# Two channel quarters of one block go by one-pass products of halves, with the rest of a handwritten order rearranged

## The chip, the cores and the metric

One core of a Trainium2 chip runs the whole program in one launch. The metric is the device time of an execution in microseconds; the kernel before took 228.07 us in the median of three runs (226.97 to 228.76). The core's engines are TensorE (PE, with its weight loads as PEld), VectorE (DVE), ScalarE (ACT), GpSimd (POOL) and SyncE (SP), which issues the DMAs here.

## The reference, cut to what matters

A state-space scan over 4 batches of 8 heads, 768 tokens, is followed by a token mixer of rank 32 and a channel mixer. In the second part, per batch,

```
h  = x.T @ U @ V                    # 768 -> 32 -> 768 over tokens
u  = x + h.T                        # (768, 256)
ch = relu(u @ w_ch1) @ w_ch2        # 256 -> 1024 -> 256
out = u + ch                        # float32
```

and x is the scan's output with heads and head channels put side by side. The weights arrive as float64 and are turned into float32 on the chip.

## The kernel before, in words

Everything is issued in the order of one string, PLAN. Each word is a letter with indices, and calls one small function; the engines take their instructions in that order, each in a queue of its own, with semaphores between them where data or buffers require it. No time stands in the plan.

The scan goes by 12 pairs of 128-token blocks, three pairs a batch. For pair k: `L` loads its B, C and x (SP; a load is held until the last VectorE instruction ahead of it in the plan is done), `P` scales B and C (VectorE), `T` transposes them (TensorE, then three ScalarE copies; two words), `g` forms the products C·B in four PSUM banks, `m` and `M` mask two of these banks each (VectorE), `s` and `u` update the state (TensorE; VectorE, then a GpSimd multiplication, L567), `n` is the part inside a chunk (L633), `i` and `j` the two parts from the state (L611). Before `j` a one-column GpSimd copy (L574, tile `settled`) waits for the products of `n` and `i`, and the products of `j` wait for that copy. `y` takes the result from PSUM (two ScalarE copies), `t` transposes it to tokens.

The mixer of batch b has `p`, `q` and `a` (rank-32 token mixing; `a` ends in two VectorE additions into u), and then a channel mixer by blocks j of 384 tokens, channels m of 128 (8 of them, in four quarters of two), and output blocks k of 128 tokens:

- Batches 1 to 3 use halves. A number x is split into near = x·(1 - 2^-13) rounded to fp32r, far = x - near, and a third operand joined from both. `S` does so for u (a ScalarE copy at L722, two VectorE passes over 128x768). `f` (four products and a ScalarE scaling, L732) and `e` (two products and a ScalarE relu into near, L761) make one channel of the first layer; `h` takes far from PSUM and, after each second channel, joins (VectorE). `d b.j.k.n` is piece n of six of the second layer: near, far and joined halves against the three forms of the weights, four channels a piece, with a scaling of the bank after piece 3 and a product for the mixed tokens, an addition and the output's DMA after piece 5.
- Batch 0 uses plain float32: `U` makes a channel of the first layer into a tile gT (relu by ScalarE, L744), and `d` has four pieces, one quarter (two channels) each. All products of both kinds are issued at L727.

Weights: `c` (three steps) turns a tile of words into float32, `R` (two steps for w_ch1, three for w_ch2; R4 to R7 are the quarters of w_ch2) makes the three forms. The third form of a w_ch2 quarter takes the place of its float32 form, so R's third step must come after the last plain product with that quarter.

PSUM has two banks for each of the tags w, x, y and z. `f`, `U` and `a` use x or z, `g` two of each, a `d` block one (x, z, x for k = 0, 1, 2; y in the last three blocks). A bank is used again after `h` (for f and e), the mask (for g) or the addition (for d and a) has read it. All VectorE instructions carry line L158, that of a recording helper.

Of the kernel before, what the change touches and what calls it, by code (L numbers as in the profile page):

```python
# [22 lines left out]
AF = mybir.ActivationFunctionType
ALU = mybir.AluOpType
# [16 lines left out]
    'c0 i3 c2 b5.2 b5.0 q0 P4 j3 y3 W2 W3 b5.1 W4 a0.0 c2 a0.1 T4 T4 w5 c3 c3 c3 x4.0 U0.0.0 P5 '  # L41
    'U0.0.1 U0.1.1 R0 B6 t3 X5 g4 m4 T5 M4 T5 c5 c5 U0.1.0 c5 X6 U0.1.3 c4 c4 s4 u4 w6 w7 w8 U0.0.3 '
    'P6 U0.0.2 c6 U0.0.6 s5 c4 U0.1.7 c6 U0.1.2 u5 R0 R2 U0.1.6 n4 s6 L7 i4 g5 c6 R4 j4 y4 u6 T6 T6 '
    'm5 R2 R1 U0.0.4 M5 U0.1.4 n5 i5 L8 g6 c7 c7 c9 c9 j5 P7 T7 T7 M6 c7 t4 y5 U0.0.7 c8 U0.0.5 t5 '
    'm6 n6 R3 c9 P8 c8 p1 R7 g7 m7 L9 i6 M7 T8 T8 c8 q1 d0.0.2.0 d0.0.2.1 U0.1.5 a1.1 R1 d0.0.2.2 '
    'd0.0.2.3 a1.0 d0.0.1.0 R3 d0.0.1.1 d0.0.1.2 d0.0.0.0 d0.0.0.1 S1.0 f1.0.0 R7 d0.0.0.2 f1.0.1 '
    'd0.0.0.3 e1.0.0 h1.0.0 R5 d0.0.1.3 f1.0.6 R6 e1.0.1 d0.1.0.0 f1.0.7 P9 d0.1.0.1 h1.0.1 e1.0.6 '
    'd0.1.0.2 L10 R6 h1.0.6 e1.0.7 s7 u7 h1.0.7 f1.0.3 f1.0.2 d0.1.0.3 e1.0.2 d0.1.1.0 P10 h1.0.2 '
    'e1.0.3 h1.0.3 d0.1.2.0 f1.0.4 d0.1.1.1 R4 R4 f1.0.5 d0.1.1.2 d0.1.1.3 e1.0.4 e1.0.5 d0.1.2.1 '
    'd0.1.2.2 h1.0.4 h1.0.5 R6 d0.1.2.3 s8 j6 g8 y6 u8 s9 m8 n7 i7 S1.1 f1.1.0 f1.1.2 j7 y7 u9 M8 '  # L50
    't6 R5 e1.1.0 h1.1.0 n8 i8 T9 T9 t7 R5 d1.0.1.0 d1.0.1.1 d1.0.1.2 d1.0.0.0 d1.0.0.1 d1.0.0.2 '
    'd1.0.0.3 e1.1.2 R7 f1.1.3 d1.0.0.4 d1.0.0.5 d1.0.1.3 j8 y8 s10 d1.0.2.0 e1.1.3 h1.1.2 h1.1.3 '
# [12 lines left out]
    'f3.0.6 e3.0.0 h3.0.0 e3.0.1 d2.1.1.0 f3.0.3 d2.1.1.1 d2.1.1.2 d2.1.1.3 h3.0.1 f3.0.2 d2.1.1.4 '
    'e3.0.6 h3.0.6 e3.0.2 h3.0.2 d2.1.1.5 e3.0.3 h3.0.3 d2.1.0.5 f3.0.4 f3.0.5 f3.0.7 e3.0.4 h3.0.4 '
    'e3.0.5 d3.0.2.0 e3.0.7 d3.0.1.0 d3.0.2.1 d3.0.2.2 h3.0.5 d3.0.1.1 d3.0.1.2 S3.1 f3.1.4 f3.1.1 '
    'h3.0.7 d3.0.2.3 d3.0.1.3 f3.1.0 e3.1.4 h3.1.4 d3.0.2.4 e3.1.0 d3.0.2.5 e3.1.1 f3.1.5 d3.0.0.0 '
    'f3.1.2 d3.0.0.1 d3.0.0.2 d3.0.0.3 e3.1.2 h3.1.0 h3.1.1 f3.1.3 e3.1.5 h3.1.5 h3.1.2 d3.0.0.4 '
    'f3.1.6 e3.1.3 h3.1.3 d3.0.0.5 f3.1.7 d3.0.1.4 d3.0.1.5 e3.1.6 h3.1.6 e3.1.7 h3.1.7 d3.1.1.0 '  # L70
    'd3.1.1.1 d3.1.1.2 d3.1.1.3 d3.1.2.0 d3.1.2.1 d3.1.1.4 d3.1.1.5 d3.1.2.2 d3.1.2.3 d3.1.0.0 '
    'd3.1.0.1 d3.1.0.2 d3.1.0.3 d3.1.2.4 d3.1.2.5 d3.1.0.4 d3.1.0.5 ')


@with_exitstack
def kernel(
# [27 lines left out]
    nc = tc.nc  # L104
    P = 128
# [12 lines left out]
    NQ = NM // 2  # L118
# [28 lines left out]
    class Kept:  # L147
# [15 lines left out]
    vector = Kept(nc.vector)  # L163
# [7 lines left out]
        out=a_sb,  # L171
# [51 lines left out]
    w2f, w2b = {}, {}  # L223
# [102 lines left out]
    R = NB * NH * NC // 2  # L326
    la_ps = bank("w", 2, R)
    for g in range(2):
# [3 lines left out]
        out=la.rearrange("p b c h -> p b h c"),  # L332
        in0=la_ps.rearrange("p g (b h c) -> p (g b) h c", h=NH, c=NC),
# [337 lines left out]
    def mixer(b):  # L671
# [59 lines left out]
        def scaled(t):  # L731
            nc.scalar.activation(t, t, AF.Copy, scale=1.0 + EPS)  # L732
# [30 lines left out]
        def third(j, m):  # L763
# [5 lines left out]
            if m % 2:  # L769
                joined(near, far, both)  # L770

        def down(j, k, n):

            parts = b or j >= PLAIN
            pieces = 6 if parts else 4

            def weight(v, m):
                return w2[v][:, m] if v < 2 else w2b[m // 2][:, m % 2]

            if n == 0:  # L780
                gs["o", j, k] = bank(TAGS.get((b, j), "xzx")[k], DM)
            t = gs["o", j, k]
            c = HS // P * j + k
            if parts:
                v, half = divmod(n, 2)
                products(t, [(gs[j, m // 2][v][:, m % 2, ts(k, P)], weight(v, m))
                             for m in range(NQ * half, NQ * half + NQ)], n == 0)
                if n == 3:
                    scaled(t)
            else:  # L790
                products(t, [(gT[j, n][:, m, ts(k, P)], w2f[n][:, m]) for m in range(2)], n == 0)
            if n == pieces - 1:
# [57 lines left out]
    def ytokens_kept(k):  # L850
# [61 lines left out]
```

## Time and profile before

| | |
|---|---|
| median of three runs | 228.07 us |
| profiled execution: time, span | 227.86 us, 226.1 us |
| TensorE: matmuls, busy | 3012, 216.1 us (96%) |
| VectorE, ScalarE, GpSimd busy | 157.6, 114.3, 14.3 us |
| granted TensorE clock | 1.00 throughout |
| chain that ended last: TensorE's share | 89% |
| HBM read, written | 10.98 MB, 3.15 MB |

The span runs from the first instruction to the last; the time has a little around it. "Busy" unites overlapping instructions, and matmuls overlap in the profile, so the step from one matmul's start to the next is the better measure of what it costs. The plan's words can be told in the time line by their tiles: `x<-w2c,words` is a down piece of plain float32 (or of joined halves later), `x<-u,w` belongs to f or e, `y<-T,Sm` to i or j, `y<-M,x` to n. Waits are told as "idle before, and who ended it".

### The profile page before, as it was taken

The page shows a single profiled execution, that of the slowest core. Times are in us where ns is not written, and L with a number is a line of the kernel's source. Part 1 is how long each engine was busy: PE and PEld are TensorE (multiplying, and loading weights), DVE is VectorE, ACT ScalarE, POOL GpSimd, SP SyncE. Part 2 cuts the span into 40 slices and gives each one's busy share as a digit, 9 for nine tenths or more (in the row PEclk, how much of TensorE's full clock was granted, in tenths as well). Part 3 has the DMA queues.
Part 4 walks back from the last instruction along what each step waited for, and adds up shares of the span by engine and source line. Part 5 has one row for each costly group of instructions (what it writes and reads, how often), then busy time and mean ns, then how long its engine had stood idle before and what let it go on. Part 6 is the DMA issues. An engine that isn't in the chain of part 4 may idle for free.

```text
span 226.1 us, 7010 instructions
## 1 busy us (share of the span) xinstructions
PE 216.1 (96%) x3012; PEld 182.6 (81%) x3012; DVE 157.6 (70%) x331; ACT 114.3 (51%) x260; POOL 14.3 (6%) x37
## 2 busy tenths in 40 slices
PE   7889889999999999999999999999999999999993
PEld 4556645556678898997899898897998999999993
DVE  4675789899998866969816775667447974774921
ACT  3334856866995446333544532466237545655410
POOL 3020110012100000202101000100000000000000
PEclk9999999999999999999999999999999999999999
DMA  6997996887654402600001602000010000100011
GB/s 85 126 102 151 157 160 196 158 155 243 86 78 53 69 4 61 100 23 26 3 26 36 107 0 73 3 3 3 1 53 19 0 0 26 46 0 28 28 42 46
DMA packets 69518, 14.56 MB, mean 64 GB/s; under 512 B 63792, under 2 KB 67696, under 8 KB 69488
## 3 DMA queue, kind: packets, MB, share of 16 engines
q1 hardware_dynamic: 69488, 14.13, 34.0%
q8 instruction: 23, 0.38, 0.7%
q14 instruction: 7, 0.06, 0.1%
HBM read 10.98 MB, written 3.15 MB: 62 GB/s over the span
## 4 chain that ended last, share of the span: by engine, by line
PE 89%; DVE 3%; SPq 2%; DMA 2%; ACT 1%; issue 1%; POOL 0%; DVEq 0%; POOLq 0%
PE x L727 31%; PE z L727 24%; PE y L727 12%; PE y L633 4%; PE y L611 4%; PE x L509 2%; PE w L478 2%; SPq L184 2%; PE w L654 2%; PE z L509 2%; DMA bc<-in_B_dram 2%; PE w L681 1%; PE w L541 1%; DVE S L158 1%; PE w L689 1%
## 5 line engine op out<-in xcount | busy, mean ns | idle before, releaser
L158 DVE SCALAR_TENSOR_TENSOR words<-words 128x768 fp32r<-128x768 f32 (+6 forms) x44 | 34.7, 806 | 1.9 <-ACT words L415 0.6
L727 PE MATMUL z<-u,w 128*128 128x384 f32 x144 | 34.0, 350 | 0.0
L727 PE MATMUL x<-u,w 128*128 128x384 f32 x144 | 33.2, 348 | 0.0
L732 ACT ACTIVATE x<-x 128x384 f32<-128x384 f32 (+1 forms) x30 | 13.6, 452 | 25.2 <-PE x L727 25.1
L727 PEld LDWEIGHTS z<-u,w 128*128 128x128 f32 x144 | 24.6, 188 | 1.3 <-DVE words L158 0.2
L727 PEld LDWEIGHTS x<-u,w 128*128 128x128 f32 x144 | 24.0, 188 | 1.3 <-ACT x L732 0.6
L158 DVE SCALAR_TENSOR_TENSOR words<-x,words 128x384 fp32r<-128x384 f32 x24 | 13.3, 556 | 16.4 <-ACT words L761 13.7
L727 PE MATMUL x<-w2c,words 128*128 128x256 f32 x112 | 22.5, 338 | 0.0
L732 ACT ACTIVATE z<-z 128x384 f32<-128x384 f32 (+1 forms) x27 | 12.5, 463 | 14.2 <-PE z L727 13.6
L727 PEld LDWEIGHTS x<-w2c,words 128*128 128x128 f32 x112 | 18.2, 189 | 1.3
L727 PE MATMUL y<-w,words 128*128 128x256 f32 x144 | 19.1, 282 | 0.0
L727 PEld LDWEIGHTS y<-w,words 128*128 128x128 f32 x144 | 18.5, 188 | 0.3 <-DVE ytok L158 0.3
L158 DVE SCALAR_TENSOR_TENSOR words<-z,words 128x384 fp32r<-128x384 f32 x24 | 13.2, 552 | 5.7 <-ACT words L761 5.7
L761 ACT ACTIVATE words<-x 128x384 fp32r<-128x384 f32 x24 | 11.7, 490 | 6.3 <-PE x L727 6.2
L761 ACT ACTIVATE words<-z 128x384 fp32r<-128x384 f32 x24 | 11.6, 491 | 4.9 <-PE z L727 4.8
L567 POOL TENSOR_TENSOR Sm<-S,own 128x256 f32<-128x256 f32 (+1 forms) x12 | 7.7, 644 | 89.9 <-DVE S L158 60.3
L646 ACT COPY yT<-y 128x256 f32<-128x256 f32 x24 | 7.8, 381 | 10.5 <-PE y L611 10.2
L158 DVE SCALAR_TENSOR_TENSOR S<-S,kept,w 128x64 f32<-128x64 f32 x40 | 11.2, 280 | 2.7 <-PE w L541 1.0
L611 PE MATMUL y<-T,Sm 32*64 32x64 f32 x352 | 12.4, 240 | 0.6 <-POOL Sm L567 0.3
L727 PE MATMUL x<-w,words 128*128 128x256 f32 x96 | 12.6, 282 | 0.0
L158 DVE TENSOR_TENSOR M<-x,causal 128x256 int32<-128x256 int32 x24 | 9.0, 418 | 5.0 <-PE x L509 2.6
L509 PE MATMUL x<-Cm,T 32*64 32x128 f32 x192 | 11.4, 307 | 0.9 <-ACT Cm L488 0.7
(149 smaller groups left out, 403.4 us busy)
## 6 DMA issues: line engine op xcount, KB each, us to landing
words<-in_moe_w_ch_dram SPq DMA_DIRECT2D x7, 512.0 KB, 5.9
x<-in_x_dram SPq DMA_DIRECT2D x24, 128.0 KB, 3.8
out_dram<-ytok SPq DMA_DIRECT2D x24, 128.0 KB, 1.7
bc<-in_B_dram SPq DMA_DIRECT2D x24, 64.0 KB, 3.8
bc<-in_C_dram SPq DMA_DIRECT2D x12, 128.0 KB, 3.7
words<-in_moe_w_ch_dram SPq DMA_DIRECT2D x2, 256.0 KB, 4.6
words<-in_moe_V_dram SPq DMA_DIRECT2D x4, 48.0 KB, 2.7
words<-in_moe_U_dram SPq DMA_DIRECT2D x1, 192.0 KB, 4.0
```

What stands on the lines that cost most here:

```text
L158: self.last = call(*args, **kwargs)
L184: op = nc.sync.dma_start(**kwargs)
L478: nc.tensor.transpose(out=tp[:, i, v], in_=s["BC"][:, i, c + v].rearrange("p h n -> p (h n)"), identity=ident)
L509: nc.tensor.matmul(out=g[r][cols, c], lhsT=s["T"][rows, 0, c, cols], rhs=s["Cm"][rows, :, :, ts(2 * c + p, Q)].rearrange("r v t i -> r v i ...
L567: nc.gpsimd.tensor_tensor(out=s["Sm"][:, sl], in0=s["S"][:, sl].rearrange("p i (s d) -> p i s d", s=2), in1=own2[:, b, 4 * q + sl.start:4 ...
L611: product = nc.tensor.matmul(out=y[p][ts(r % 2, H), r // 2, c], lhsT=own[ts(r, Q)], rhs=s["T"][ts(r, Q), 1, :, ts(2 * c + p, Q)].rearrange ...
L633: product = nc.tensor.matmul(out=y[p][ts(i, Q), n, c], lhsT=x_sb[k][half, c, h], rhs=s["M"][half, h // 2, c, h % 2], start=fresh(k, p, [i] ...
L646: nc.scalar.copy(out=yp[:, :, :, p], in_=st[k]["y"][p])
L654: nc.tensor.transpose(out=t[:, c, g], in_=yT[b][:, g, ts(2 * q + c, P)], identity=ident)
L727: nc.tensor.matmul(out=t, lhsT=lhsT, rhs=rhs, start=start, stop=True, skip_group_check=True)
L732: nc.scalar.activation(t, t, AF.Copy, scale=1.0 + EPS)
L761: nc.scalar.activation(gs[j, m // 2][0][:, m % 2], t, AF.Relu, scale=NEAR)
```

## The change: what it does

In batch 0's second block (j = 1), quarters 0 and 3 of the second layer are no longer multiplied in plain float32. A new word `G` halves their gT tile: its first step is a ScalarE copy of 128x768 into near, its second two VectorE passes of 128x768 (far, joined). A block's `d` still has four pieces: piece 0 is now eight one-pass products (near and far of channels 0, 1, 6, 7) and a scaling of the bank, piece 1 four (joined), and pieces 2 and 3 the plain quarters 1 and 2. The first block (j = 0) stays plain.

The plan is the same up to the second `c9`, at pair 5; behind it the same words, and four `G`, stand in another order to the end. Among the moves: R4 and R7 end beside the block's first pieces; a1.0 before a1.1, and S1.0 between them; L10 before L9; j6 before batch 1's first e; j7 right behind g8; i9 before g9; i10 before M10, and s11 behind g11; a2.1 into batch 1; j11 shortly behind n11.

```diff
+ONE_PASS = (0,3)
...
-    'm5 R2 R1 U0.0.4 M5 U0.1.4 n5 i5 L8 g6 c7 c7 c9 c9 j5 P7 T7 T7 M6 c7 t4 y5 U0.0.7 c8 U0.0.5 t5 '
-    'm6 n6 R3 c9 P8 c8 p1 R7 g7 m7 L9 i6 M7 T8 T8 c8 q1 d0.0.2.0 d0.0.2.1 U0.1.5 a1.1 R1 d0.0.2.2 '
-    'd0.0.2.3 a1.0 d0.0.1.0 R3 d0.0.1.1 d0.0.1.2 d0.0.0.0 d0.0.0.1 S1.0 f1.0.0 R7 d0.0.0.2 f1.0.1 '
-    'd0.0.0.3 e1.0.0 h1.0.0 R5 d0.0.1.3 f1.0.6 R6 e1.0.1 d0.1.0.0 f1.0.7 P9 d0.1.0.1 h1.0.1 e1.0.6 '
-    'd0.1.0.2 L10 R6 h1.0.6 e1.0.7 s7 u7 h1.0.7 f1.0.3 f1.0.2 d0.1.0.3 e1.0.2 d0.1.1.0 P10 h1.0.2 '
-    'e1.0.3 h1.0.3 d0.1.2.0 f1.0.4 d0.1.1.1 R4 R4 f1.0.5 d0.1.1.2 d0.1.1.3 e1.0.4 e1.0.5 d0.1.2.1 '
-    'd0.1.2.2 h1.0.4 h1.0.5 R6 d0.1.2.3 s8 j6 g8 y6 u8 s9 m8 n7 i7 S1.1 f1.1.0 f1.1.2 j7 y7 u9 M8 '
-    't6 R5 e1.1.0 h1.1.0 n8 i8 T9 T9 t7 R5 d1.0.1.0 d1.0.1.1 d1.0.1.2 d1.0.0.0 d1.0.0.1 d1.0.0.2 '
...
-    'T11 T11 M9 i9 n9 g10 m10 M10 j9 y9 s11 u11 i10 g11 m11 M11 n10 f2.0.4 a2.1 f2.0.3 f2.0.2 '
-    'e2.0.4 h2.0.4 e2.0.3 e2.0.2 f2.0.7 f2.0.6 h2.0.2 h2.0.3 f2.0.0 f2.0.1 e2.0.0 e2.0.7 e2.0.1 '
-    'h2.0.0 h2.0.1 j10 y10 t9 e2.0.6 h2.0.6 h2.0.7 f2.0.5 i11 n11 e2.0.5 h2.0.5 d2.0.1.0 d2.0.0.0 '
-    'd2.0.0.1 d2.0.0.2 d2.0.0.3 d2.0.1.1 d2.0.1.2 d2.0.1.3 S2.1 d2.0.0.4 d2.0.0.5 d2.0.1.4 d2.0.1.5 '
...
-    'd3.1.1.1 d3.1.1.2 d3.1.1.3 d3.1.2.0 d3.1.2.1 d3.1.1.4 d3.1.1.5 d3.1.2.2 d3.1.2.3 d3.1.0.0 '
-    'd3.1.0.1 d3.1.0.2 d3.1.0.3 d3.1.2.4 d3.1.2.5 d3.1.0.4 d3.1.0.5 ')
+    'm5 R2 R1 U0.0.4 M5 U0.1.4 n5 i5 L8 g6 c7 c7 c9 c9 R3 j5 y5 P7 t4 M6 c7 m6 U0.0.7 t5 U0.0.5 c9 '
+    'T7 T7 p1 c8 c8 n6 g7 i6 P8 m7 c8 G0 M7 T8 T8 d0.0.2.0 q1 R7 d0.0.2.1 R1 d0.0.2.2 d0.0.2.3 R7 '
+    'U0.1.5 a1.0 R3 d0.0.0.0 S1.0 G3 R4 a1.1 G0 d0.0.0.1 d0.0.0.2 L10 d0.0.1.0 d0.0.1.1 d0.0.1.2 '
+    'd0.0.0.3 f1.0.1 d0.0.1.3 j6 R6 s7 G3 R7 d0.1.0.0 f1.0.0 R4 d0.1.1.0 e1.0.0 d0.1.0.1 d0.1.1.1 '
+    'h1.0.0 R5 e1.0.1 u7 d0.1.1.2 f1.0.6 h1.0.1 d0.1.1.3 f1.0.7 d0.1.0.2 e1.0.6 e1.0.7 R6 h1.0.6 L9 '
+    'f1.0.3 d0.1.0.3 h1.0.7 f1.0.2 d0.1.2.0 e1.0.2 e1.0.3 h1.0.2 h1.0.3 f1.0.5 P9 d0.1.2.1 f1.0.4 '
+    'P10 d0.1.2.2 e1.0.5 s8 u8 e1.0.4 y6 h1.0.4 d0.1.2.3 h1.0.5 T9 T9 R5 n7 i7 g8 j7 y7 m8 M8 t6 '
+    'd1.0.0.0 S1.1 L11 d1.0.0.1 d1.0.0.2 d1.0.1.0 d1.0.1.1 f1.1.0 s9 u9 n8 i8 t7 R5 e1.1.0 d1.0.1.2 '
...
+    'T10 i9 g9 m9 T10 T11 T11 M9 n9 g10 m10 j9 y9 i10 M10 g11 m11 s11 u11 n10 f2.0.4 M11 f2.0.2 '
+    'f2.0.3 e2.0.4 h2.0.4 e2.0.2 f2.0.7 e2.0.3 h2.0.2 h2.0.3 f2.0.6 j10 y10 t9 e2.0.6 e2.0.7 h2.0.6 '
+    'h2.0.7 f2.0.0 f2.0.5 f2.0.1 e2.0.0 h2.0.0 e2.0.5 i11 h2.0.5 n11 e2.0.1 h2.0.1 S2.1 j11 y11 t10 '
+    'd2.0.1.0 d2.0.1.1 d2.0.0.0 d2.0.0.1 d2.0.0.2 d2.0.0.3 f2.1.3 d2.0.0.4 f2.1.2 d2.0.1.2 d2.0.0.5 '
...
+    'h3.1.6 e3.1.7 d3.1.2.0 d3.1.2.1 d3.1.1.1 h3.1.7 d3.1.1.2 d3.1.1.3 d3.1.2.2 d3.1.2.3 d3.1.1.4 '
+    'd3.1.1.5 d3.1.2.4 d3.1.0.0 d3.1.0.1 d3.1.0.2 d3.1.0.3 d3.1.2.5 d3.1.0.4 d3.1.0.5 ')
...
             if m % 2:
                 joined(near, far, both)
 
+        def halved(j, q):
+
+            g, near = gT[j, q], pair(FP32R)
+            nc.scalar.activation(near, g, AF.Copy, scale=NEAR)
+            yield
+            gs[j, q] = [near, pair(FP32R), pair(FP32R)]
+            vector.tensor_tensor(out=gs[j, q][1], in0=g, in1=near.bitcast(FP32), op=ALU.subtract)
+            joined(*gs[j, q])
+            yield
+
+        def mixed(j):
+
+            few = [(v, m) for v in range(3) for q in ONE_PASS for m in (2 * q, 2 * q + 1)]
+            full = [q for q in range(NQ) if q not in ONE_PASS]
+            n = NQ - len(full)
+            cuts = {2: [8, 12], 3: [6, 12, 18], 4: [8, 16, 20, 24]}[n]
+            parts = [few[a:c] for a, c in zip([0, *cuts], cuts)]
+            return parts + [[(None, q)] for q in full], cuts.index(4 * n)
+
         def down(j, k, n):
 
             parts = b or j >= PLAIN
...
                              for m in range(NQ * half, NQ * half + NQ)], n == 0)
                 if n == 3:
                     scaled(t)
+            elif j and ONE_PASS:
+                cut, last = mixed(j)
+                products(t, [pq for v, m in cut[n] for pq in (
+                    [(gT[j, m][:, i, ts(k, P)], w2f[m][:, i]) for i in range(2)] if v is None else
+                    [(gs[j, m // 2][v][:, m % 2, ts(k, P)], weight(v, m))])], n == 0)
+                if n == last:
+                    scaled(t)
             else:
                 products(t, [(gT[j, n][:, m, ts(k, P)], w2f[n][:, m]) for m in range(2)], n == 0)
             if n == pieces - 1:
...
 
         us, gs, gT = {}, {}, {}
         return SimpleNamespace(p=project, q=parted, a=added, S=split, f=first, e=second, h=third,
-                               d=down, U=plain)
+                               d=down, U=plain, G=halved)
 
 
     assert HS // 2 == NC * RK
...
     mx = {0: mixer(0)}
 
 
-    finer, turns = {}, {}
+    finer, turns, halving = {}, {}, {}
 
     def refined(c):
 
         next(finer.setdefault(c, refine(c)))
+
+    def parted_hidden(q):
+
+        next(halving.setdefault(q, mx[0].G(1, q)))
 
     def turned(k):
 
...
                  j=lambda k: inter(k, 1), y=yout, t=ytokens, L=load, Q=lambda k, c: prep(k, c, 1),
                  O=ytokens_of, o=ytokens_kept,
                  V=lambda k, c, v: turn(k, c, 1, "wx"[v // 2], vector if v % 2 else None))
-    whole = dict(c=convert, R=refined, A=lambda i: decays(every_batch, "w", [i]),
+    whole = dict(c=convert, R=refined, G=parted_hidden, A=lambda i: decays(every_batch, "w", [i]),
                  K=lambda n: keep(every_batch, "z"), F=lambda n, tag: warm(n, "wxzy"[tag]),
                  v=lambda n: spread())
```

## The prediction

> **What bounds the kernel now.** I read the page from the top: first the busy shares, then the slices, then the chain that ended last.
>
> ```profile
> span 226.1 us, 7010 instructions
> ...
> PE 216.1 (96%) x3012; PEld 182.6 (81%) x3012; DVE 157.6 (70%) x331; ACT 114.3 (51%) x260; POOL 14.3 (6%) x37
> ...
> PE   7889889999999999999999999999999999999993
> ...
> PEclk9999999999999999999999999999999999999999
> ...
> PE 89%; DVE 3%; SPq 2%; DMA 2%; ACT 1%; issue 1%; POOL 0%; DVEq 0%; POOLq 0%
> ```
>
> TensorE is busy in every slice from 30 us on, at the full granted clock, and is 89% of the chain. So a microsecond of its work taken away is worth one, and a wait put into its queue costs one. But "busy" includes short waits, since ends are modelled; what counts is the distance between matmul starts. Next I read those, in the time line of TensorE alone (columns: start, length, engine, line, operation, tiles, shape, count).
>
> ```profile
> 75.63 2.75 PE L727 MATMUL z<-w2c,words 128*128 128x256 f32 x12
> 78.22 1.89 PE L727 MATMUL x<-w2c,words 128*128 128x256 f32 x8
> ...
> 131.54 1.58 PE L727 MATMUL z<-w,words 128*128 128x256 f32 x12
> 132.96 2.53 PE L727 MATMUL x<-w,words 128*128 128x256 f32 x20
> ```
>
> The first two rows are the plain down product of batch 0. Each product is two matmul instructions, so 12 are 6 products in 78.22 - 75.63 = 2.59 us, **0.432 us a product**. The last two rows are one-pass products of a later batch: 12 in 132.96 - 131.54 = 1.42 us, **0.118 us each**.
>
> Laid on the plan word by word, the starts give f 0.70 us, e 0.35, a plain down piece 0.866, a one-pass piece 0.47. By these steps the matmuls from j5 (62.08 us) to the end need 154.2 us and took 222.5 - 62.1 = 160.4, so 6.2 us is lost there. About 3 of it lies in changes of shape (0.02 to 0.05 us a word). The rest are waits: g9 0.48, g11 0.55, i9 0.25, i6 and a1.1 0.24, f2.0.5 0.21, and a dozen of 0.1 to 0.2.
>
> **The work that goes and comes.** For each of three token blocks k, channel quarters 0 and 3 lose 4 plain products, 12 in all: 12 x 0.432 = 5.18 us. They gain 3 halves x 4 channels = 12 one-pass products a block, 36 in all: 36 x 0.118 = 4.25 us. TensorE: **-0.93 us**. The weights' refinements (R4 to R7) are the same, only earlier.
>
> Three scalings of a bank (0.36 us, from the 128x256 rows of L732) come onto ScalarE. Between piece 0 and piece 1 of a block stand other pieces of 1 to 5 us, so they cost nothing; with nothing between, 0.6 us each.
>
> Two halvings come, G0 and G3: one ScalarE copy of 128x768 each (L722: 0.84 us) and two VectorE passes of 0.96 us. ScalarE's 1.7 us lies in its idle time. VectorE's 3.8 us does not, since they fall where it is the fullest:
>
> ```profile
> 62.10:70.10 8.00, 8.00 (x175) 6.03 (x168) 7.59 (x17) 7.56 (x18) 0.00 (x0) 1.00 0.42 57
> 70.10:78.20 8.10, 8.10 (x38) 6.86 (x37) 7.30 (x14) 2.94 (x7) 0.00 (x0) 1.00 0.58 84
> 78.20:86.20 8.00, 8.00 (x42) 7.39 (x41) 4.63 (x8) 4.24 (x9) 0.00 (x0) 1.00 0.07 24
> ```
>
> (Windows; columns after the length: PE, PEld, DVE, ACT, POOL, clock, DMA.) VectorE has 0.4 us of 8 free, then 0.8, then 3.4. From P7 to d0.0.0.2 the new plan hands it 22.9 us beside 15.6 us of matmuls; the old one hands it 17.7 in the same stretch, with R4, R7 and the halvings after it or absent.
>
> **The stage from 62 to 108 us, walked by hand** with these rows' durations. VectorE keeps the old order up to m7 (69.7), ends c8 at 71.7 (d0.0.2.2 wants it at 71.9), M7 at 72.3, the adds of a1.0 at 76.4. S1.0 then waits on ScalarE, behind R3, until 78.5, and ends at 80.4; R4 81.0, the adds of a1.1 82.0, G0 83.9. TensorE reaches f1.0.1 at 81.85, and the z bank is free when a1.1 is added: **+0.25**. d0.1.0.0 starts at 84.5; its last two products read G3's far half, ready at 85.5 because the adds of d0.0.0.3 and d0.0.1.3 stand before it: **+0.35**. d0.1.0.1 (87.8) needs the weights of R7 and R4, ready at 87.0 and 87.7: just in time. L9's loads now wait for h1.0.6 (94.8). With about 1.5 us of issue and 3.8 us to land, P9 can start at 100.2, with its T9 at 102.8: covered. If that cover went, P10, u8 and the bank releases h1.0.4 and h1.0.5 behind P9 would hold g8. L10 comes earlier and blocks nothing on SP that is due.
>
> **The reordered waits.** A second part of inter (j) waits for a tiny GpSimd copy, which waits for n and i. That copy is the row to read, beside the VectorE row at the same time:
>
> ```profile
> 92.06 1.07 DVE L158 SCALAR_TENSOR_TENSOR words<-words 128x768 fp32r<-128x768 f32 x1
> ...
> 92.26 0.92 POOL L574 COPY settled<-slot 128x1 f32<-128x1 f32 x1
> 110.19 0.18 POOL L574 COPY settled<-slot 128x1 f32<-128x1 f32 x1 [1.43 <-PE y L611]
> ```
>
> Alone it takes 0.18 us, beside a VectorE pass with two SBUF inputs 0.92 (0.94 at 105.94): it ends when that pass ends. In the old plan 1.4 us of f stand between i7 and j7, and 10 us between n11 and j11. In the new one only g8 (0.6) and e2.0.1 (0.35) do, while the join of h1.0.5 and that of h2.0.5 run. j7: 0 to 0.9, taken **+0.2** (the join ends as g8 does). j11: n11's end + 1.05 against + 0.35, between 0.1 (no pass in the way) and 0.9, taken **+0.7**. [...] Without such a hold the sum would be 0.8 us lower.
>
> Others: d3.1.0.0 takes the y bank 0.47 us after d3.1.1.5 where the add needs 0.67 (+0.2; covered by 0.94 before); d3.1.0.4 and p2 +0.15. In the g9 to f2.0.4 stretch i9 now fills g9's wait, but s11 no longer fills g11's: 0. Waits that go: the three e that stood 0.70 us behind their f (0.1 to 0.2 each), f2.0.5, e1.1.0, e2.1.5 and some of e1.0.7, i6 and a1.1: -1.2, with 0 to -2 as ends, since what is late next is always another e within 0.1 us.
>
> **Sum.** -0.93 + 0.25 + 0.35 + 0.2 + 0.7 + 0.35 - 1.2 = -0.28 us: a span of 225.8, a time of 227.86 - 0.28 = 227.6. That execution (226.1 us of span, 227.86 in all) lies 0.21 under the median of 228.07. I forecast **227.7 us**, no change that can be told: 1% (2.3 us) is about what a measurement of this kernel can tell from none, as its three runs lie 1.8 us apart.
>
> **Rivals.**
> - *The reordering pays in full*: VectorE keeps up, j11 doesn't wait, and more of the 3 us of waits goes. For it: nearly every bank's release has more room in the new order. Against: 22.9 us of VectorE work beside 15.6. Work -0.93, waits -2 to -0.5: 225.0 to 226.5, about 225.8. Chance 0.22; some 0.11 lies beyond 1%.
> - *VectorE's queue becomes the bound* (slower than before): my walk lets passes that follow each other overlap by 0.07 us as the rows do (73.47, 73.94). Where each waits for the last, as the 0.99 us between the starts at 79.10 and 80.09, G0 ends at 85.4, not 83.9, and f1.0.1, d0.0.0's bank, G3 and d0.1.0.0 move with it: +1.5, and as much again if S1.0's copy on ScalarE is behind R3 and G0 too. It decides once VectorE is 0.5 us later than walked; 229.2 to 231.0, chance 0.24, of which 0.14 beyond 1%.
> - *The change doesn't save what it says*: one-pass products as single pieces in between f32 ones may take the 0.19 us that f words show behind plain pieces (79.76: 0.88 for 0.70). Plain pieces in front are 0.19 shorter there, so it should be no loss. If it is, at six joints +1.1: 228.8. Chance 0.09.
>
> **How the numbers follow.** Forecast 0.45 (227.0 to 228.5), full gain 0.22, VectorE 0.24, no saving 0.09. The range leaves out the lowest tenth of the gains and the highest tenth of the VectorE case: **225.7 to 230.0**. Faster by over 1% 0.11, slower by over 1% 0.14, else 0.75.
>
> **What would show it.** Step 1: the 36 new products at 0.118 us and 12 plain ones fewer. Step 2: in the time line f1.0.1 and d0.1.0.0 start late, with VectorE without a gap from 62 to 85 us. Step 3: the settled copy of j11 lasting near 0.9 us, and TensorE idle or stretched before j11. Step 4: d3.1.0.0 waiting for a VectorE add. The prediction is wrong if d0.1.0.1 waits for R4 by over 1 us, if P9 comes later than T9, or if the banks held by h and M are late in batches 2 and 3, whose order I compared only by the room between words.

## The result and the profile after

The changed kernel took **229.49 us** in the median of 13 runs (228.68 to 230.13), the kernel before 227.49 us (13 runs beside them): a ratio of **1.0081, 95% interval 1.0062 to 1.0100**. A second series of the same two kernels gave 1.0072 (1.0054 to 1.0090). So the change makes the kernel slower by 0.8%, where I had forecast no difference. A few executions of any of these kernels run at a lower granted clock, the profiled ones of e1_front (0.985) and e9_mix (0.978) among them; the ratios leave them out.

The profiled execution took 229.56 us (span 227.3), 1.70 us more than the one before (227.86). These lines of its page answer to those shown of before:

```profile
span 227.3 us, 7043 instructions
...
PE 215.7 (95%) x3024; PEld 181.7 (80%) x3024; DVE 161.5 (71%) x335; ACT 117.5 (52%) x265; POOL 14.5 (6%) x37
...
PEclk9999999999999999999999999999999999999999
...
q8 instruction: 24, 0.39, 0.8%
...
PE 87%; ACT 3%; SPq 2%; DVE 2%; DMA 2%; issue 2%; POOL 1%; POOLq 0%; DVEq 0%; ACTq 0%
```

TensorE has less work (215.7 us busy against 216.1, though in 3024 matmuls instead of 3012) in a longer span, and its share of the chain falls from 89% to 87%, while "issue" is 2% instead of 1% (88% and 1% in its second execution, below). The clock is full in both. So TensorE waits more. What it waits for is in the view of waits; these are the rows of TensorE's matmuls in the changed kernel that before doesn't have, or has smaller (columns: total us, times, longest):

```profile
PE y L612 <- POOL settled L575: 1.3, 3, 0.6
...
PE y L634 <- issue: 0.7, 1, 0.7
...
PE y L612 <- ACT yT L647: 0.5, 1, 0.5
```

The same rows of the kernel before (its lines are one number lower) are a single wait for the settled copy, and "issue" in nothing but two short pauses of g, 0.27 us at 15.29 and 0.19 at 20.29 (the first is shown):

```profile
PE x L509 <- issue: 0.3, 1, 0.3
PE y L611 <- POOL settled L574: 0.3, 1, 0.3
```

Where they stand is seen in TensorE's time line of the changed kernel:

```profile
86.25 1.10 PE L728 MATMUL z<-w,words 128*128 128x256 f32 x8
87.19 0.52 PE L728 MATMUL x<-u,w 128*128 128x384 f32 x2
...
105.53 0.50 PE L612 MATMUL y<-T,Sm 32*64 32x64 f32 x16 [0.42 <-POOL settled L575]
...
143.30 0.57 PE L612 MATMUL y<-T,Sm 32*64 32x64 f32 x8 [0.49 <-ACT yT L647]
...
146.58 0.27 PE L634 MATMUL y<-M,x 64*32 64x64 f32 x2 [0.68 <-issue]
...
158.73 0.50 PE L612 MATMUL y<-T,Sm 32*64 32x64 f32 x16 [0.59 <-POOL settled L575]
```

The first two rows are the new product: eight one-pass products in 87.19 - 86.25 = 0.94 us, 0.118 each. The other four are waits of j7, i10, n10 and j11. The one of n10 is odd: it stands inside n10, ahead of its last two matmuls (one product), no semaphore event ends it ("issue"), and nothing was known of it before.

**A balance by stages.** I laid the plan's words on TensorE's time line and took from each word's step (its start to the next word's start) the step that such a word needs undisturbed, as in the prediction (f 0.70, e 0.35, plain piece 0.866 and so on). What is left is lost time. The table counts it from g6, where the orders part, to the last matmul; the stretch itself is 154.8 us of work plus the loss where all products of batch 0 are plain, 153.9 where two quarters go by one-pass products. It leaves out the start, which varies by itself between executions. All numbers are us, of one profiled execution each.

| kernel | stretch | lost | g6 to i7 | to q2 | to T10 | to n10 | to the end |
|---|---|---|---|---|---|---|---|
| before | 161.14 | 6.31 | 1.21 | 0.85 | 0.85 | 1.14 | 2.26 |
| changed | 163.09 | 9.21 | 1.68 | 1.34 | 0.65 | 2.45 | 3.09 |
| changed, second execution | 162.53 | 8.64 | 1.66 | 0.84 | 0.64 | 2.51 | 2.99 |
| e16_front2 | 161.72 | 6.89 | 1.62 | 1.12 | 0.82 | 1.14 | 2.19 |
| e15_order2 | 162.81 | 7.98 | 1.62 | 1.14 | 0.64 | 1.51 | 3.07 |
| e13_i10far | 161.12 | 7.23 | 1.65 | 0.82 | 0.82 | 1.54 | 2.40 |
| e7_s11late | 162.55 | 8.66 | 1.67 | 1.42 | 0.66 | 1.61 | 3.30 |
| e6_pad24 | 162.44 | 7.61 | 1.20 | 0.84 | 0.84 | 2.50 | 2.23 |

The lost time rises from 6.31 to 9.21 us, by 2.90, and the work falls by 0.93: a stretch longer by 1.95. The part ahead of g6, which the change doesn't touch, happened to be 0.44 shorter in this execution, so the last matmul ends 1.52 later (224.02 against 222.50). The rise sits in two places above all: T10 to n10 (+1.31) and behind n10 (+0.83).

### The profile page after: what moved, and what is told of

It is laid out like the page before. It is cut to its first block, busy times and chain, and to the rows that moved or that the text cites. A ratio compares the mean times of both kernels' runs of the same rounds, so it can differ in the third digit from the quotient of the medians.

```text
span 227.3 us, 7043 instructions
## 1 busy us (share of the span) xinstructions
PE 215.7 (95%) x3024; PEld 181.7 (80%) x3024; DVE 161.5 (71%) x335; ACT 117.5 (52%) x265; POOL 14.5 (6%) x37
## 4 chain that ended last, share of the span: by engine, by line
PE 87%; ACT 3%; SPq 2%; DVE 2%; DMA 2%; issue 2%; POOL 1%; POOLq 0%; DVEq 0%; ACTq 0%
PE x L728 30%; PE z L728 22%; PE y L728 12%; PE y L634 4%; PE y L612 4%; SPq L185 2%; PE w L479 2%; PE x L510 2%; PE w L655 2%; DMA bc<-in_B_dram 2%; PE w L542 1%; PE z L510 1%; PE w L682 1%; DVE S L159 1%; PE w L690 1%
## 5 line engine op out<-in xcount | busy, mean ns | idle before, releaser
L159 DVE SCALAR_TENSOR_TENSOR words<-words 128x768 fp32r<-128x768 f32 (+6 forms) x46 | 36.5, 811 | 2.0 <-ACT words L416 0.6
L728 PE MATMUL z<-u,w 128*128 128x384 f32 x144 | 33.2, 342 | 0.0
L728 PEld LDWEIGHTS z<-u,w 128*128 128x128 f32 x144 | 23.9, 188 | 1.0 <-DVE words L159 0.5
L728 PE MATMUL x<-w2c,words 128*128 128x256 f32 x104 | 20.3, 327 | 0.0
L728 PE MATMUL y<-w,words 128*128 128x256 f32 x144 | 19.9, 283 | 0.0
L728 PEld LDWEIGHTS x<-w2c,words 128*128 128x128 f32 x104 | 16.6, 189 | 1.2 <-DVE w2c L159 0.2
L728 PE MATMUL x<-w,words 128*128 128x256 f32 x112 | 15.6, 284 | 0.0
L728 PEld LDWEIGHTS x<-w,words 128*128 128x128 f32 x112 | 14.3, 188 | 0.3
L612 PEld LDWEIGHTS y<-T,Sm 32*64 32x64 f32 x352 | 8.6, 131 | 6.4 <-POOL settled L575 2.9
L634 PE MATMUL y<-M,x 64*32 64x64 f32 x768 | 11.6, 224 | 1.2 <-issue 0.7
```

The costliest lines, as they stand in the source:

```text
L159: self.last = call(*args, **kwargs)
L612: product = nc.tensor.matmul(out=y[p][ts(r % 2, H), r // 2, c], lhsT=own[ts(r, Q)], rhs=s["T"][ts(r, Q), 1, :, ts(2 * c + p, Q)].rearrange ...
L634: product = nc.tensor.matmul(out=y[p][ts(i, Q), n, c], lhsT=x_sb[k][half, c, h], rhs=s["M"][half, h // 2, c, h % 2], start=fresh(k, p, [i] ...
L728: nc.tensor.matmul(out=t, lhsT=lhsT, rhs=rhs, start=start, stop=True, skip_group_check=True)
```

## The experiments

Theories at the start: (A) the new order behind T10 brings waits of its own; (B) VectorE is overfilled where the halves are made; and, from the fifth run on, (C) TensorE's own code.

### Halves of the order, and the covers

Four kernels beside each other. The first has the changed plan up to T10 and the old plan behind it, the second the reverse with plain products:

```diff
 e1_front:  PLAN = <changed, up to T10> + <before, from T10, without a2.1>
 e2_back:   PLAN = <before, up to T10, a2.1 set between a2.0 and S2.0> + <changed, from T10>;  ONE_PASS = ()
```

> The changed kernel up to the word T10 (138 us: one-pass products, halvings, all of the new order of batches 0 and 1), and behind it the old order. Theory A (the waits of the new order behind T10 cost the time; ahead of it saved work and new waits cancel, since the TensorE starts of the two traces lose 0.94 us more there and the work is 0.93 less): within 0.4 us of the kernel before, 227.5. Theory B (the rival: the halvings overfill VectorE between 62 and 86 us, and that is the loss): all of the loss is here, 229.5.

> The complement: the old order and plain products up to T10 (only a2.1 is moved ahead, to behind a2.0, since the new tail expects it there), and behind it the new order. Theory A: the loss is here, +1.5 to +2.0 us over the kernel before, 229.2. Theory B: no loss, 227.5 or a little less.

e1_front: 229.37 us, ratio 1.0072 (1.0057 to 1.0086). e2_back: 230.12 us, 1.0105 (1.0056 to 1.0153). Each half alone seems as slow as the whole, so no simple sum of A and B fits. In e2_back 1.2 of it is my own edit, a2.1 straight behind a2.0:

```profile
131.72 0.44 PE L700 MATMUL x<-Vs,ps 128*128 128x384 f32 x1 [0.84 <-DVE yT L159]
```

The loss from q2 to T10 is 2.08 us there against 0.85. In e1_front the order behind T10 is the old one, and yet n10 has the pause again:

```profile
150.05 0.30 PE L634 MATMUL y<-M,x 64*32 64x64 f32 x3 [1.49 <-issue]
```

The third kernel gives three words their old cover back:

```diff
-i7 g8 j7 y7 m8 M8 t6 d1.0.0.0 S1.1 L11 d1.0.0.1 d1.0.0.2
+i7 g8 m8 M8 t6 d1.0.0.0 S1.1 L11 d1.0.0.1 d1.0.0.2 j7 y7
-j9 y9 i10 M10 g11 m11 s11 u11 n10
+j9 y9 s11 i10 M10 g11 m11 u11 n10
-S2.1 j11 y11 t10 d2.0.1.0 d2.0.1.1 d2.0.0.0 d2.0.0.1
+S2.1 t10 d2.0.1.0 d2.0.1.1 d2.0.0.0 d2.0.0.1 j11 y11
```

> The changed kernel with three covers given back: j7 and y7 stand behind d1.0.0.2, j11 and y11 behind d2.0.0.1, and s11 stands between y9 and i10 as before. Theory A: the waits of TensorE there (0.5 before j7, 0.5 before i10, 0.8 before j11 in the changed kernel's trace) go, 1.5 to 1.8 us less than the changed kernel, 227.8; the settled copies may still last 0.9 us, unseen. Theory B: the waits are moved, not removed, since VectorE is late anyway; 229.0 to 229.5.

229.46 us, ratio 1.0080 (1.0071 to 1.0088): no gain at all. The waits for the settled copy are gone and so is i10's, but t6 waits 0.41 longer, d2.0.1.0 0.38, and what was won ahead of n10 is lost in it:

```profile
146.74 0.30 PE L634 MATMUL y<-M,x 64*32 64x64 f32 x3 [1.13 <-issue]
```

It ends at 146.74, where the changed kernel's ended at 146.58, although TensorE came to it 0.29 earlier (146.74 - 1.13 against 146.58 - 0.68). In these two executions n10's pause works like a gate that opens at nearly the same time, whenever TensorE comes to it.

The fourth sets the halves into the old order (G0 and G3 ahead of d0.0.0.1, the last steps of R7 and R4 ahead of d0.1.0.1):

```diff
-d0.0.0.1 S1.0 f1.0.0 R7 d0.0.0.2 ... R6 e1.0.1 d0.1.0.0 f1.0.7 P9 d0.1.0.1
+G0 G3 d0.0.0.1 S1.0 f1.0.0 R7 G0 d0.0.0.2 ... R6 e1.0.1 R4 G3 f1.0.7 h1.0.1 s7 e1.0.6 d0.1.0.0 R7 R4
```

> The work alone: the old order, with the one-pass products, the halvings and the earlier R4 and R7 set into it between 78 and 97 us (some pieces of d0.1 and some f, e, h there stand up to a few places elsewhere; nothing behind 100 us is moved). Theory A: the saved 0.93 us of TensorE shows, less small waits: 226.5 to 227.0, faster than both. Theory B: VectorE's 3.8 us more in this stage hold TensorE up: 228.5 to 229.5. Third possibility, the one-pass pieces save nothing: 227.5.

234.32 us, ratio 1.0301 (1.0248 to 1.0353). TensorE's time line shows what the halves cost where nobody made room for them:

```profile
80.38 0.62 PE L728 MATMUL x<-u,w 128*128 128x384 f32 x2 [0.48 <-ACT u L723]
81.37 0.62 PE L728 MATMUL x<-u,w 128*128 128x384 f32 x2 [0.37 <-DVE u L159]
...
91.67 1.58 PE L728 MATMUL x<-w2c,words 128*128 128x256 f32 x8 [1.14 <-DVE w2c L159]
...
97.39 0.62 PE L728 MATMUL x<-u,w 128*128 128x384 f32 x2 [1.52 <-ACT x L733]
```

The halves' copies stand ahead of S1.0 on ScalarE, and the refinements are late on VectorE: 7.05 us lost up to i7 against 1.21. So mechanism B is real, but the changed kernel's order avoids it (1.68 lost up to i7). And n10 pauses again (1.33 us).

### The pause in n10: theory C, TensorE's code

So far the pause stood in every kernel with one-pass products and in neither with plain ones (before, e2_back). Two things differ between these: the work, and the count of instructions. 36 one-pass products in place of 12 plain ones (two matmul instructions each) are 12 matmuls and 12 weight loads more, 24 entries in TensorE's stream. The profile has a queue "q8 instruction", which moves 16 KB packets (0.39 MB in 24), and 6,048 matmuls and loads over 24 packets make one packet for some 252 entries. I took these packets for the code of TensorE's stream; no record says so. In the changed kernel one packet runs from 144.23 to 145.19 us. These two lines are from the view of the DMA queues for 144.0 to 145.3 us:

```profile
DMA packets 1, 0.02 MB, mean 13 GB/s; under 512 B 0, under 2 KB 0, under 8 KB 0
...
q8 instruction: 1, 0.02, 4.6%
```

No other DMA is under way, and from 145.3 to 147 there is none at all. n10 goes on at 146.58, 1.39 us after the packet. In e3_covers it is 1.32 after one, in e1_front 1.43, in e5_work 1.33. Theory C: a border between two blocks of code falls behind n10's 62nd matmul of 64, at the end of a dense stretch (360 short entries from g10 on, a load and a matmul for each of the 180 matmuls of g10, j9, i10, g11, s11 and n10), and TensorE has used up the old block before the new one can be used.

The test puts 24 entries into the kernel before without any work: five warm-up words at the start are cut finer, the same idle columns in more instructions.

```diff
-x1.1 F2.0 A0 ... A1 F2.1 ... b3.0 F2.1 ... m1 F3.0 M1 ... c0 F2.3 v0
+x1.1 F1.0 F1.0 A0 ... A1 F1.1 F1.1 ... b3.0 F1.1 F1.1 ... m1 F1.0 F1.0 F1.0 M1 ... c0 F1.3 F1.3 v0
```

> The kernel before with five warm-up words at the start split into finer ones (the same idle columns in seven matmul instructions instead of one to three columns each: 24 more TensorE entries, loads counted), nothing else changed; all work and its order are those of before. Theory C, TensorE's code fetch: the 24 entries that the one-pass pieces add shift the border between two 16 KB code blocks into n10, and TensorE pauses there until the fetched block is usable. It expects a pause marked issue of 0.7 to 1.5 us in n10 near 146 us, no other change, and 228.2 to 229.0 us (ratio 1.003 to 1.007). Rival, the order of the words: nothing changes (ratio 1.000, no pause in n10).

**230.23 us, ratio 1.0120 (1.0089 to 1.0152)**: as much as the whole change or more, for 24 entries. Its waits:

```profile
PE y L633 <- issue: 1.1, 1, 1.1
...
PE y L137 <- issue: 1.0, 1, 1.0
...
PE w L689 <- issue: 0.6, 1, 0.6
```

The pause in n10 is there (1.08 us, 1.45 after a packet's end), as theory C says, and two that I had not expected, at 29.40 us (0.95) and 34.42 (0.60), 1.42 and 1.57 after a packet: by theory C the borders near the start have moved as well. 1.08 + 0.95 + 0.60 = 2.63 us is nearly the 2.8 us by which the medians differ; the match is a rough one, since the profiled execution (231.63 us) lies 1.4 above its median. The only words near n10 are the old ones, so the pause is no matter of the new order.

The next kernel takes entries away from the stretch instead: s11 and u11 go behind n10, into long products.

```diff
-M10 g11 m11 s11 u11 n10 f2.0.4 M11 f2.0.2 f2.0.3
+M10 g11 m11 n10 f2.0.4 M11 f2.0.2 s11 f2.0.3 u11
```

> The changed kernel with s11 moved behind f2.0.2 and u11 behind f2.0.3: 48 short TensorE entries leave the dense stretch ahead of n10's end. Theory C (code fetch) expects that n10's pause (0.68 us in the changed kernel) goes and no pause marked issue takes its place, because the block's border now falls among long products: 0.6 to 1.0 us less than the changed kernel, so 228.5 to 228.9 us (ratio 1.004 to 1.006). The rival (the pause is a wait for VectorE's masks or the like) expects the pause to stay in n10 or in f2.0.4 behind it: ratio 1.008.

229.18 us, ratio 1.0065 (1.0041 to 1.0089); 0.84 us less is lost from T10 to n10 than in the changed kernel. n10 runs through:

```profile
145.13 0.86 PE L634 MATMUL y<-M,x 64*32 64x64 f32 x64
145.92 1.66 PE L728 MATMUL x<-u,w 128*128 128x384 f32 x8
147.51 0.43 PE L542 MATMUL w<-x,BC 64*32 64x64 f32 x24
```

The time fell by less than I expected, and by no more than the intervals allow (1.0081 and 1.0065 overlap); the pause's going is shown, its worth of 0.6 to 1.0 us in the whole time is not.

The reverse by entries alone, three warm-up words dropped, the columns of two of them given to others (12 entries fewer):

```diff
-... A1 F2.1 ... K0 F1.3 ... m1 F3.0 ... Q2.2 F1.0 ... c0 F2.3 v0
+... A1 F3.1 ... K0 ... m1 F4.0 ... Q2.2 ... c0 v0
```

> The changed kernel with three warm-up words at the start dropped and their idle columns given to two others (12 TensorE entries fewer, loads counted), the rest untouched. Theory C, the code fetch: the block's border moves from the last two products of n10 to behind the first long products of the next word, so the pause marked issue in n10 goes and nothing else near it moves: 0.5 to 0.8 us less than the changed kernel, 228.5 to 229.0 us, ratio 1.003 to 1.006, unless the shifted borders bring a pause between 25 and 40 us. Rival (the pause belongs to n10's own place in the order): pause and ratio (1.007 to 1.008) as in the changed kernel.

229.00 us, ratio 1.0071 (1.0046 to 1.0096): a miss. The pause did leave n10, but it moved on instead of going, and another came at 30.49 us:

```profile
PE y L847 <- issue: 0.8, 1, 0.8
...
PE x L728 <- issue: 0.5, 1, 0.5
```

The second stands at 148.91 us inside f2.0.2, 1.47 after a packet. That the pause travels with the entry count and is shorter among long products (0.5 us in f2.0.2 against 0.68 in n10) speaks for C; that shifting all borders is a way to win does not follow.

A count of TensorE's recorded matmuls (each has one weight load) shows where the pauses stand. The pause in n10 stands behind 2,380 to 2,384 matmuls in all six executions that have it, and e11_less12's in f2.0.2 behind 2,385, although the words there are others. The pauses near 30 us stand behind 602 (in e6_pad24 and e11_less12 alike) and 729, the two short ones of g in the kernel before behind 221 and 347. All of these lie, to within 5, at 221 plus a multiple of 127, and 127 matmuls with their loads are 254 entries, by theory C a block of code, with a border at each of these places. The packets that had ended by then were 1, 2, 4, 5 and 18, one for each border so far.

How dense is too dense, the count bounds only in part. In the six executions the 127 matmuls ahead of the border in n10 ran in 2.3 to 2.8 us, and TensorE went on 3.0 to 3.9 us after the border before; in the kernel before, e7_s11late, e13_i10far and e16_front2 the same block takes 3.9 us and more, and there is no pause. But the block ahead of that one runs in 2.15 us in the kernel before (140.96 to 143.11) and ends in no pause; its packet had started at 140.62, ahead of the block, while the packet for n10's border in the changed kernel started 0.6 us into it (144.23 against 143.59).

### What bounds the stretch around j7

The covers again, now with the pause away, and then i10 moved behind m11 besides:

```diff
 e8_best:  e3_covers with s11 and u11 placed as in e7_s11late
 e10_i10:  e8_best, and
-j9 y9 i10 M10 g11 m11 n10
+j9 y9 M10 g11 m11 i10 n10
```

> The changed kernel with j7 and y7 behind d1.0.0.2, j11 and y11 behind d2.0.0.1 (as in e3_covers), and s11 behind f2.0.2, u11 behind f2.0.3 (as in e7_s11late). Theory C: the code fetch was a gate that swallowed what the covers of e3_covers saved; with the gate away the covers pay: 0.4 to 0.8 us less than e7_s11late and 1.0 to 1.3 less than e3_covers, 228.0 to 228.5 us. Theory A without the gate (covers do nothing): as e7_s11late.

> e8_best with i10 moved behind m11, away from the two yT copies that j9's bank waits for. If i10's wait for ScalarE (0.49 us in the changed kernel) is a loss of its own, 0.3 to 0.5 us less than e8_best: 228.3 to 228.6 us (ratio 1.004 to 1.006). If VectorE's masks bound the stretch from g9 to n10 anyway, the wait moves to g11 and nothing is saved (ratio 1.006).

e8_best: 228.85 us, ratio 1.0063 (1.0039 to 1.0086). e10_i10: 229.06 us, 1.0066 (1.0050 to 1.0083). Against e7_s11late (1.0065) neither shows a gain. By the steps the cover of j11 is worth 0.32 us (2.98 lost behind n10 against 3.30), that of j7 nothing (1.47 against 1.42 from i7 to q2), and i10's move made the stretch to n10 longer (1.88 against 1.61), with g11's step at 1.26 instead of 1.15. One more kernel moves t6 and j7 together and has the old order behind T10:

```diff
-g8 j7 y7 m8 M8 t6 d1.0.0.0 S1.1 L11 d1.0.0.1 d1.0.0.2 d1.0.1.0 d1.0.1.1
+g8 m8 M8 d1.0.0.0 S1.1 L11 d1.0.0.1 d1.0.0.2 j7 y7 d1.0.1.0 d1.0.1.1 t6
 <from T10: the old order, i10 behind m11, s11 behind f2.0.4, u11 behind f2.0.3>
```

> The changed kernel once more, unedited, as the yardstick of this chip for the two kernels beside it. Every theory: ratio 1.006 to 1.010; theory C (TensorE's code fetch) also expects the pause marked issue in n10 again, 0.6 to 1.1 us long and ending 1.3 to 1.6 us after a 16 KB instruction packet ended.

> The changed kernel up to T10 with j7, y7 behind d1.0.0.2 and t6 behind d1.0.1.1; the old order behind T10, with s11 and u11 behind f2.0.4 and f2.0.3 and i10 behind m11. If the loss is the sum of the new order's waits behind T10, the pause in n10 and the two waits about j7, and the one-pass pieces save 0.93 us, it lies 2.0 to 2.6 us under the changed kernel: 226.8 to 227.6 us (ratio 0.997 to 1.001). If one-pass products save nothing, 227.8 to 228.6 us.

The changed kernel once more: 229.23 us, 1.0072 (1.0054 to 1.0090), pause in n10 0.75 us, 1.44 after a packet. e9_mix: 230.01 us, 1.0109 (1.0071 to 1.0147), a plain miss: I had expected a time no worse than before. The reason can be read in its time line, TensorE's row first, then VectorE's for the same moment:

```profile
109.40 1.68 PE L728 MATMUL x<-w,words 128*128 128x256 f32 x12 [0.74 <-DVE M L159]
```

```profile
106.84 0.55 DVE L159 SCALAR_TENSOR_TENSOR words<-z,words 128x384 fp32r<-128x384 f32 x1
107.43 0.96 DVE L159 SCALAR_TENSOR_TENSOR words<-words 128x768 fp32r<-128x768 f32 x1
108.30 0.71 DVE L159 TENSOR_TENSOR words<-w2c,w 128x512 f32<-128x512 f32 x1
108.94 0.74 DVE L159 TENSOR_TENSOR M<-x,causal 128x256 int32<-128x256 int32 x2
```

d1.0.0.0 takes a bank of g8, which m8 must read first, and m8 stands behind h1.0.5's two passes and R5's in VectorE's queue, which is full: in the changed kernel it has no gap over 0.15 us from 98.2 to 107.3. In e3_covers, e8_best, e10_i10 and the second execution of the changed kernel, too, d1.0.0.0 starts 0.46 to 0.47 us after m8 does, as here (109.40 against 108.94). Whether j7 or t6 is put between g8 and that bank, the wait is VectorE's. That is why the cover of j7 bought nothing here.

### The order by itself

The changed order with plain products only, whole and up to T10 (old order behind). At first R4's and R7's last steps, which must come after the last plain piece of their quarters, stood behind d0.1.2.3:

```diff
 e4_order:       changed PLAN without G; ONE_PASS = (); last R4 and R7 behind d0.1.2.3
 e14_frontplain: the same up to T10, old order behind
```

> The changed kernel's order alone: all of batch 0's second block plain again (no halving, R4's and R7's last steps behind the block's last piece), so TensorE has 0.93 us more work than the changed kernel and 24 entries fewer. If the new order's own waits are the loss (theory A) it stays at 1.5 to 2 us above the changed kernel less the early-stage waits for halves: 229.4 to 230.4 us (ratio 1.008 to 1.013), without a pause in n10. Theory B (VectorE and ScalarE overfilled by halving) expects 0.5 to 1 us lost less between 62 and 100 us than in the changed kernel, 228.6 to 229.2 us. Theory C expects no pause in n10, so 0.7 us less than the sum of theory A.

> The changed kernel's order up to T10 with plain products only (no halving; R4's and R7's last steps behind the block's last piece), the old order behind. The order's part ahead of T10 alone, without one-pass products and without the 24 entries. By the sums of TensorE's steps in e4_order (1.4 of 2.7 us up to T10) it is 1.2 to 1.8 us slower than before: 228.6 to 229.3 us (ratio 1.005 to 1.008). If the loss lies behind T10 alone, as before (ratio 1.000).

e4_order: 230.71 us, ratio 1.0139 (1.0116 to 1.0162), more than any theory expected; e14_frontplain: 228.98 us, 1.0064 (1.0043 to 1.0084). Neither pauses in n10. But 2.1 us are lost between i7 and q2, more than in the changed kernel: the two late steps stand ahead of m8 in the queue just shown. So they were placed again, R4's behind d0.1.2.0, R7's behind d1.0.0.3:

> As e4_order (the changed kernel's order, plain products, no halving), but R4's last step behind d0.1.2.0 and R7's behind d1.0.0.3, away from the stretch ahead of g8 where e4_order had put both. Order theory: without that placement the new order alone costs 1.8 to 2.1 us of TensorE's waiting, 229.4 to 229.9 us (ratio 1.008 to 1.010) and no pause in n10. If those two passes were the order's whole loss, 228.0 us or less.

> As e14_frontplain (new order up to T10, plain products, old order behind) with R4's and R7's last steps placed as in e15_order2. The new order up to T10 alone then costs 0.6 to 0.9 us: 228.2 to 228.6 us (ratio 1.002 to 1.005), and the difference to e15_order2, 1.1 to 1.3 us, is what the new order behind T10 costs. If e14_frontplain's loss was that placement alone, ratio 1.000.

e15_order2: 229.36 us, **1.0105 (1.0074 to 1.0136)**. e16_front2: 227.80 us, **1.0033 (1.0021 to 1.0046)**. By the steps: the new order costs 6.89 - 6.31 = **0.58 us up to T10** and 7.98 - 6.89 = **1.09 us behind it**, 1.67 in all, without one product changed (one execution each, with R4's and R7's last steps not where the changed kernel has them). The part behind T10 is 0.37 up to n10 (i10 and n9 wait where s11 and i9 stood) and 0.88 to the end, less 0.18 from q2 to T10 (the second of T10's words, with g9 and i9 ahead of it). j11's settled copy is the largest of it: e2.0.1's step is 0.86 too long in this kernel too.

Last, what the one-pass products save where no pause follows them: e1_front with 32 short entries, i10, moved out of the stretch ahead of n10's end.

```diff
-j9 y9 s11 u11 i10 g11 m11 M11 n10 f2.0.4 f2.0.3
+j9 y9 s11 u11 g11 m11 M11 n10 f2.0.4 i10 f2.0.3
```

> e1_front (changed kernel up to T10, old order behind) with i10 moved behind f2.0.4: 32 short entries leave the stretch ahead of n10's end. Theory C: no pause in n10 (1.49 us in e1_front), and if the old order behind T10 then costs what it did, about the time before: 227.2 to 228.0 us (ratio 0.999 to 1.003). If the order up to T10 alone is the loss, 228.5 us or more.

228.44 us, ratio **1.0018 (0.9985 to 1.0052)**, no pause in n10: the changed products without a measurable loss. Its stretch is 161.12 us against 161.72 in e16_front2, which has the same order up to T10 with plain products: 0.60 us less, and as long as before (161.14). The two differ behind T10 by i10's place as well, so the part up to T10 is the fairer comparison: 76.93 us against 78.15, **1.2 us less with one-pass products**, and 0.7 and 1.2 less in the two executions of the changed kernel than in e15_order2, around the 0.93 of the sum; i10's place costs the other 0.6. By the whole time (1.0018 and 1.0033) the intervals overlap, and no saving is shown. Against e1_front, which differs by i10's place alone, the ratio falls from 1.0072 (1.0057 to 1.0086): with the pause gone the whole time is some 1.2 us shorter. No version beat the kernel before.

## Why the prediction was wrong

The sum forecast -0.93 us of work and +0.65 of waits. The work was right; the lost time rose by 2.90. By its steps:

- **The work, -0.93: right.** 0.118 us a product as read from the later batches, and the stretch up to T10 in e13_i10far against e16_front2 (1.2 us shorter) shows that it can be had. The rival "doesn't save what it says" is out.
- **The walk from 62 to 108 us: right in time, partly wrong in place.** S1.0 was walked to end at 80.4, the adds of a1.1 at 82.0, G0 at 83.9; they ended at 80.18, 81.71 and 83.57, in an execution that was 0.44 ahead. But f1.0.1 started at 81.85 without the 0.25 that I charged for the z bank, and d0.1.0.0 showed some 0.1 of its 0.35. In their place the steps of a1.0 and a1.1 were 0.29 and 0.34 too long (a1.1 was 0.24 before). The stage to i7 lost 0.47 more against 0.60 forecast. The new order alone does that (1.62 in e16_front2), so the halves, which I blamed, cost next to nothing there.
- **j7's settled copy, +0.2: undersized in one execution.** These are GpSimd's rows of the changed kernel, then of its second execution:

```profile
104.73 0.75 POOL L575 COPY settled<-slot 128x1 f32<-128x1 f32 x1 [1.66 <-PE y L612]
...
157.72 0.95 POOL L575 COPY settled<-slot 128x1 f32<-128x1 f32 x1 [10.55 <-PE y L634]
```

```profile
104.84 0.18 POOL L575 COPY settled<-slot 128x1 f32<-128x1 f32 x1 [1.65 <-PE y L612]
...
157.40 0.95 POOL L575 COPY settled<-slot 128x1 f32<-128x1 f32 x1 [10.56 <-PE y L634]
```

  At j7 the copy falls on the joint between two VectorE passes: 0.02 us before the second pass's start it took 0.75 us in the one execution and 0.18 in the other. g8's step was 0.68 too long in the first, and the stage to q2 lost 0.49 and nothing more than before. So whether the copy was held can't be told from hundredths of a start; that my 0.2 lies between the two cases is luck, since neither of them is 0.2.
- **j11's settled copy, +0.7: right.** It lasted 0.95 us beside h2.0.5's join in both, against 0.18 at j7 in the second execution, and e2.0.1's step was 0.86 too long.
- **d3.1 and p2, +0.35: roughly right**, 0.21 found, at d3.1.2.4.
- **"In the g9 to f2.0.4 stretch ...: 0": wrong, the main fault.** It was +1.31 up to n10. I had netted i9's gain against s11's loss by the words beside g, and did not ask who holds the y banks when i10 follows j9: y9's copy on ScalarE (0.49 us, in the time line above). The larger part, some 0.9 to 1.0 us, is the pause in n10, of which the forecast had no step at all. In the profile of before the queue "q8 instruction" and its 23 packets were on the page that I read; I did not ask what they could cost.
- **"Waits that go, -1.2": about two thirds right, and spent elsewhere.** Leaving the seven large ones aside (g8, e2.0.1, n10, and n9, j9, g9, g11 about T10; 4.53 in all, against 1.48 of g9, i9, s11 and g11 before), what lies over 0.1 us a word came to 2.76 us net before and 1.95 after: -0.8. But the small losses of up to 0.1 a word, changes of shape mostly by my estimate, rose from 2.07 to 2.73 with the finer interleaving. I had counted these as constant.
- **The rival "VectorE's queue becomes the bound"** named 62 to 86 us and a point of decision 0.5 us away; there the queue kept its times. The bound showed 20 us later, at m8, and in e5_work, where the order made no room. It gives no part of what separates the changed kernel from before beyond what j7 shows.

Together: order +1.67, work -0.93, pause +0.9 to 1.0, j7's copy 0 to 0.5 give +1.6 to +2.2 us; the two executions of the changed kernel show +1.95 in the stretch with j7's copy held and +1.39 without. The last 0.25 us are not resolved.

Left open: when an instruction packet is asked for, which by theory C would say how dense a stretch may be (in the kernel before, each from the seventh on starts within 2 us of TensorE's passing the border before its own; in the changed kernel some start 4 to 5 us after it); and what ends the longer steps of a1.0 and a1.1.

## What to carry to other kernels

Count instructions, not only their time: the changed kernel ran 360 short entries back to back on TensorE up to n10's end, and 24 entries without any work, added to the kernel before, brought a pause of 1.08 us into n10 (e6_pad24). Look for "issue" ahead of an instruction in the midst of a uniform row, and for an instruction packet that ended shortly before (1.32 to 1.57 us here). The 0.29 us saved ahead of the pause in e3_covers were lost in it, and moving short work behind long products took it away (e7_s11late, e13_i10far). And before a wait is given a cover, follow the releaser's queue: where the next word waited for the same queue, the cover bought nothing (j7: 1.47 us lost from i7 to q2 with it in e8_best, 1.42 without it in e7_s11late).

## What the runs showed of the hardware

TensorE paused where no semaphore event ended its wait ("issue"). In the profiles of these kernels the pauses of this kind ahead of its matmuls with 0.6 us or more (in n10 of five kernels and of the second execution, and three near 30 us in e6_pad24 and e11_less12) ended 1.32 to 1.57 us after a 16 KB packet of the instruction queue had ended, and lasted 0.6 to 1.5 us. They stand at fixed counts of TensorE's matmuls, within 5 of 221 plus a multiple of 127 (602, 729, 2,380 to 2,384), whatever work stands there. The packets took 0.88 to 1.61 us in 46 of 47 cases of the kernel before and the changed kernel, and 2.07 in one. 24 entries without work cost 1.2% of the time in one kernel (e6_pad24, 1.0089 to 1.0152).

That the packets carry TensorE's code is my reading of their count (one for some 252 of its entries) and of the fixed places of the pauses; no record says so. By that reading a dense row of short products used its instructions up before the next packet served it: the blocks of 127 matmuls that ended in a pause in n10 had run in 2.3 to 2.8 us. How early the packet starts seems to matter as well: one block of 2.15 us in the kernel before, whose packet had started 0.34 us ahead of it (140.62 against 140.96), ended in none.
